# Decode attention block with MLP: V, w1 and w2 loaded through ScalarE's DMA queue, K, wq and wo through SyncE's

## The chip, the cores and the metric

The kernel runs on one core of one Trainium2 chip. The metric is the device time of one execution in microseconds. The kernel before took 678.72 us (median of 3 runs, 678.62 to 679.22). Besides these runs there is one profiled execution of 679.1 us, from which all rows below come.

## The reference

One decode step (one token for each of 4 batch entries) of a pre-layernorm transformer block: cached attention with 32 heads of 128, over 4096 cached positions, and then an MLP with mish as its activation. All inputs are bf16.

```python
# x: [4, 1, 640]; k_cache, v_cache: [4, 32, 4096, 128]; wq: [640, 4096]; wo: [4096, 640]
# w1: [640, 1728]; b1: [1728]; w2: [1728, 640]
q = layernorm(x) @ wq                              # 32 heads of 128
scores = einsum("bhqd,bhkd->bhqk", q, k_cache) * 128 ** -0.5
o = einsum("bhqk,bhkd->bhqd", softmax(scores), v_cache)
h = x + o.reshape(4, 1, 4096) @ wo
z = layernorm(h) @ w1 + b1
out = h + (z * tanh(softplus(z))) @ w2
```

The two caches are 134.2 MB each. With wq, wo, w1 and w2 the core reads 283.35 MB from HBM.

## The kernel before

The work is cut into 32 groups, numbered `g`. A group is one batch entry `b` and four heads (`g = 4 * hq + b`). Its K is one tile `kt` of 128 partitions by 32 KB, 4096 KB in all, and its V is one tile `vt` of the same size. Either pool has two buffers, so K of group g + 2 can only be loaded when K of group g has been used up, and V of group g + 1 only when V of group g - 1 has.

What happens in one group: VectorE multiplies the K tile in place with the broadcast query, in four pieces (L297, two halves of the tile called part 0 and part 1, two pieces each). TensorE sums the products over the head dimension by matmuls with the identity (L304), 8 for each piece. VectorE reduces the rest (`finish_sum`, L316). The softmax of group g - 1 lies in part 0 of group g: a maximum by VectorE (L327), a transpose by TensorE (L329), a maximum (L334), a broadcast (L342), and then on ScalarE a copy (L344) and four exponentials (L347). `pv(g - 1)`, 128 matmuls of 128x4 (L231), stands on TensorE behind part 1 of group g. So in group g the K tile of g is set free first, then the V tile of g - 1.

The order on each engine is that of the program text (a manual schedule). In the loop over the groups the loads stand in this order:

```python
        if g + 2 < NG:
            kts[g + 2] = load_k(g + 2)
        if 1 <= g < NG - 1:
            pv(g - 1)
        ...
        if g + 1 < NG:
            vts[g + 1] = load_v(g + 1)
```

All these loads are issued by SyncE, on one DMA queue, and so in this order: K of g + 2, V of g + 1, K of g + 3, and so on. The queue is called q1 in the profile. Each load waits on SyncE until its buffer is free. The K tile and the V tile of the last group (31) are loaded in two halves each. Between groups 8 and 11 the queue also takes wo in four pieces of 1280 KB (L392), in rows of 1280 bytes, and b1 (L397).

After the loop w1 and w2 are loaded (L421 to L425). They go into the K buffer that group 30 used. Then come the last softmax, `pv(30)`, `pv(31)`, the last product with wo (L278), the residual and a layernorm (L441 to L467), the product with w1 (L472, 70 matmuls, result `h1_ps`), the activation (L488 to L519), the product with w2 (L534, 70 matmuls), the transpose of the result (L549) and its store (L558).

ScalarE issues one DMA, the load of x (L101). Its other work is the copies of the query (L193, L207), the softmax and the activation.

Of the kernel before, what the change touches and what calls it, by code (L numbers as in the profile page):

```python
# [16 lines left out]
def kernel(  # L17
# [21 lines left out]
    nc = tc.nc  # L39
# [3 lines left out]
    F = B_w1.shape[1]  # L43
# [22 lines left out]
    FM = CK * CI * 128  # L66
    C2 = F // 128
# [8 lines left out]
    kpool = ctx.enter_context(tc.tile_pool(name="kpool", bufs=KBUFS))  # L76
    vpool = ctx.enter_context(tc.tile_pool(name="vpool", bufs=VBUFS))
# [2 lines left out]
    out_rows = out.rearrange("b s (c p) -> (b s c) p", p=128)  # L80


    def load_kv(pool, tag, cache, g):
        hq, b = divmod(g, N)
        t = pool.tile([128, R, Dh], BF16, tag=tag, name=f"{tag}{g}")
        view = cache[b, G * hq : G * (hq + 1)].rearrange("h (p r) d -> (h p) r d", p=PH)

        np_ = NP if g == NG - 1 else 1
        for i in range(np_):
            r0, r1 = i * R // np_, (i + 1) * R // np_  # L90
            nc.sync.dma_start(out=t[:, r0:r1, :], in_=view[:, r0:r1, :])
        return t

    def load_k(g):
        return load_kv(kpool, "kt", A_k_cache, g)

    def load_v(g):
        return load_kv(vpool, "vt", A_v_cache, g)

    x_bf = consts.tile([N, D], BF16)  # L100
    nc.scalar.dma_start(out=x_bf[:, :], in_=x_rows[:, :])  # L101
# [2 lines left out]
    nc.sync.dma_start(out=wq_sb[:, :, :], in_=A_wq.rearrange("(p c) n -> p c n", c=DC))  # L104
    kts, vts = {}, {}
    kts[0] = load_k(0)
    kts[1] = load_k(1)
    vts[0] = load_v(0)


    ident = consts.tile([128, 128], BF16)
# [22 lines left out]
    for q in range(G):  # L134
        nc.vector.tensor_copy(
            out=sel[:, :, q, q * PH : (q + 1) * PH],
            in_=ident[0:N, 0:N].unsqueeze(2).to_broadcast([N, N, PH]),
# [45 lines left out]
    def q_chunk(n):  # L183
        q_ps = ps.tile([N, QC], FP32, tag="qq")
        for c in range(DC):
            nc.tensor.matmul(  # L186
                q_ps[:, :],
                lhsT=xT[:, c, :],
                rhs=wq_sb[:, c, n * QC : (n + 1) * QC],
                start=(c == 0),  # L190
                stop=(c == DC - 1),
            )
        nc.scalar.copy(out=q_all[:, n * QC : (n + 1) * QC], in_=q_ps[:, :])  # L193

    def q_broadcast(hq):
        qb_ps = ps.tile([128, N * Dh], FP32, tag="qq")
        for b in range(N):
            for q in range(G):
                h = G * hq + q
                nc.tensor.matmul(  # L200
                    qb_ps[:, b * Dh : (b + 1) * Dh],
                    lhsT=sel[:, b, q, :],
                    rhs=q_all[:, h * Dh : (h + 1) * Dh],
                    start=(q == 0),
                    stop=(q == G - 1),
                )
        nc.scalar.copy(  # L207
            out=qbs[:, hq, :, :], in_=qb_ps[:, :].rearrange("p (b d) -> p b d", d=Dh)
        )
# [9 lines left out]
    for hq in Q_AT[-1]:  # L219
        q_chunk(hq)  # L220
        q_broadcast(hq)

    ot = {}

# [132 lines left out]
    for g in range(NG):  # L357
# [15 lines left out]
        if g + 2 < NG:  # L373
            kts[g + 2] = load_k(g + 2)
# [7 lines left out]
        if g + 1 < NG:  # L382
            vts[g + 1] = load_v(g + 1)
# [3 lines left out]
        if g in WO_AT:  # L387

            if not wo_sb:
# [3 lines left out]
                out=wo_sb[0][:, h0 : h0 + WOC, :],  # L393
                in_=A_wo.rearrange("(h p) n -> p h n", p=128)[:, h0 : h0 + WOC, :],
# [20 lines left out]
    w1_sb = w12[:, 0 : DC * F].rearrange("p (c f) -> p c f", c=DC)  # L415
    w2_sb = w12[:, DC * F :].rearrange("p (k i n) -> p k i n", k=CK, i=CI)
    w2s_sb = mlp.tile([128, D], BF16)
    w2r_sb = mlp.tile([FREM, D], BF16)

    w2_view = B_w2[0:FM, :].rearrange("(k p i) n -> p k i n", k=CK, i=CI)  # L420
    nc.sync.dma_start(out=w1_sb, in_=B_w1.rearrange("(c p) n -> p c n", p=128))  # L421
    nc.sync.dma_start(out=w2s_sb[:, :], in_=B_w2[FM : C2 * 128, :])
    nc.sync.dma_start(out=w2r_sb[:, :], in_=B_w2[C2 * 128 : F, :])
    for k in range(CK):
        nc.sync.dma_start(out=w2_sb[:, k], in_=w2_view[:, k])  # L425


    finish_sum(NG - 1, NP - 1)
# [26 lines left out]
    for dst in (h2T, hc):  # L455
        nc.vector.tensor_tensor(
            out=dst[:, :, :],
# [11 lines left out]
    for c in range(FC):  # L469
# [9 lines left out]
        if c == 4:  # L479
# [3 lines left out]
                out=std[:, :], in_=v_ps[:, :], func=ACT.Sqrt, bias=eps_t[:, :], scale=1.0  # L483
# [5 lines left out]
        out=h1n[:, :, :],  # L489
# [6 lines left out]
        out=h1s[:, :, :],  # L496
# [9 lines left out]
        out=tb[:, :, :],  # L506
# [8 lines left out]
        out=ta[:, :, :], in0=tb[:, :, :], scalar1=-0.5, scalar2=-1.0, op0=ALU.mult, op1=ALU.add  # L515
# [4 lines left out]
        out=act_t[:, :, :],  # L520
# [10 lines left out]
    for i, (w2, c) in enumerate(w2_of):  # L531
# [11 lines left out]
        out=oT[:, :, :].rearrange("p n c -> p c n"),  # L543
# [46 lines left out]
```

## Time and profile before

| | |
|---|---|
| the profiled execution | 679.1 us |
| its span, first to last instruction | 677.2 us |
| median of 3 runs | 678.72 us |
| bytes read from HBM | 283.35 MB |
| packets of q1 | 98.2% of the time of 16 DMA engines |
| TensorE matmuls | 467.1 us busy (69%) |
| VectorE | 352.9 us busy (52%) |
| ScalarE | 95.1 us busy (14%) |
| granted TensorE clock, mean | 0.769 |

Times in the traces are counted from the start of the span. "Busy" counts no DMA-issuing instructions. A DMA engine's share can come out slightly over 1.00, since the packets' times overlap a little at their ends. The 1.9 us between span and execution time lie before and after the instructions of the program.

### The profile page before, as it was taken

Reading aid. Unit: us, or ns where it says so; the run is one execution under the profiler, and the core shown is the slowest. Engines: PE = TensorE matmul, PEld = TensorE weight load, DVE = VectorE, ACT = ScalarE, POOL = GpSimd, SP = SyncE. Lnnn points to the kernel's source line nnn. Section 1 sums busy time; section 2 is a strip of 40 time slices with the busy share of each in tenths; the row PEclk is TensorE's granted clock in tenths of the full one; section 3 lists DMA queues with packets and bytes.
Section 4 is the critical chain, followed back from the end, with each engine's and each line's share of the span. In section 5 each row is a group of like instructions: output and inputs, shape, how many; then the busy total and the mean of one; then the engine's idle time right before and its main releaser. Section 6 shows DMA issues by size and latency. Waiting matters only on the chain.

```text
span 677.2 us, 12413 instructions
## 1 busy us (share of the span) xinstructions
PE 467.1 (69%) x5761; PEld 258.3 (38%) x5761; DVE 352.9 (52%) x304; ACT 95.1 (14%) x313; POOL 2.4 (0%) x13
## 2 busy tenths in 40 slices
PE   1588898787676475467677668767666776666965
PEld 0234445444333341343344434323333432333444
DVE  2476445456655356336654545665454566645722
ACT  0022112212101111011100111110011111101131
POOL 1000000000000000000000000000000000000000
PEclk9997678987667786687676788876788876767875
DMA  9999999999999999999999999999999999999993
GB/s 376 434 433 429 433 430 432 432 431 430 430 431 416 429 417 411 429 423 429 433 431 428 426 431 431 429 429 433 432 429 431 429 433 433 429 426 425 431 407 144
DMA packets 15211, 284.15 MB, mean 420 GB/s; under 512 B 1267, under 2 KB 5559, under 8 KB 6584
## 3 DMA queue, kind: packets, MB, share of 16 engines
q1 hardware_dynamic: 15152, 283.36, 98.2%
q8 instruction: 45, 0.74, 0.4%
q14 instruction: 6, 0.05, 0.0%
q10 hardware_dynamic: 8, 0.01, 0.0%
HBM read 283.35 MB, written 0.01 MB: 418 GB/s over the span
## 4 chain that ended last, share of the span: by engine, by line
DMA 66%; PE 16%; DVE 16%; issue 1%; ACT 0%; SPq 0%; DVEq 0%
DMA kt<-in_A_k_cache_dram 61%; PE s L304 14%; DVE kt L297 14%; DMA w<-in_B_w_dram 4%; DVE s_sb L316 2%; PE tr L329 1%; DVE mx L334 0%; PE h_ps L472 0%; PE y2T L534 0%; PE ot L231 0%; PE q_ps L186 0%; PE qb_ps L200 0%; ACT q_all L193 0%; DVE tb L517 0%; PE var_ps L449 0%
## 5 line engine op out<-in xcount | busy, mean ns | idle before, releaser
L304 PE MATMUL s<-kt,ident 128*128 128x512 bf16 x1024 | 299.5, 446 | 175.0 <-DVE kt L297 174.8
L297 DVE TENSOR_TENSOR kt<-kt,qbs 128x4096 bf16<-128x4096 bf16 x128 | 291.5, 2279 | 219.0 <-DMA kt<-in_A_k_cache_dram 219.0
L304 PEld LDWEIGHTS <-ident 128*128 128x128 bf16 x1024 | 107.8, 109 | 326.3 <-issue 178.4
L231 PEld LDWEIGHTS <-vt 128*128 128x128 bf16 x4096 | 109.0, 96 | 11.3 <-DMA vt<-in_A_v_cache_dram 2.2
L231 PE MATMUL ot<-e,vt 128*128 128x4 bf16 x4096 | 109.0, 165 | 4.0 <-DMA vt<-in_A_v_cache_dram 2.1
L347 ACT ACTIVATE e<-s_sb,nbs 32x128 bf16<-32x128 f32 x128 | 74.0, 578 | 2.5
L344 ACT COPY nbs<-tr 128x4 f32<-128x4 f32 x32 | 5.2, 162 | 467.3 <-PE tr L342 467.3
L316 DVE TENSOR_REDUCE s_sb<-s 128x64 f32<-128x512 f32 x64 | 43.5, 680 | 3.6 <-PE s L304 3.6
L347 ACT ACTIVATION_READ_ACCUMULATOR e<-s_sb,nbs 32x1 f32 x128 | 32.2, 252 | 0.0
L251 DVE RECIPROCAL rl<-l_ps 128x16 f32<-128x16 f32 x8 | 2.1, 257 | 45.3 <-PE l_ps L243 45.3
L334 DVE TENSOR_REDUCE mx<-tr 1x4 f32<-1x128 f32 x32 | 8.9, 279 | 30.5 <-PE tr L329 30.5
L186 PE MATMUL q_ps<-wq_sb,xT 128*4 128x512 bf16 x40 | 14.7, 517 | 9.2 <-DMA wq_sb<-in_A_wq_dram 9.2
L200 PE MATMUL qb_ps<-q_all,sel 4*128 4x128 bf16 x128 | 13.6, 286 | 5.3 <-ACT q_all L193 5.3
L329 PE MATMUL tr<-ident_f,pm 128*1 128x128 f32 x64 | 16.0, 344 | 1.2 <-DVE pm L327 1.2
L200 PEld LDWEIGHTS <-sel 4*128 4x128 bf16 x128 | 12.3, 128 | 10.7 <-issue 10.7
L193 ACT CAST q_all<-q_ps 4x512 bf16<-4x512 f32 x8 | 4.6, 574 | 74.6 <-PE q_ps L186 74.6
L342 PEld LDWEIGHTS tr<-mx,nscale 1*128 1x128 f32 x64 | 9.4, 183 | 13.8 <-issue 11.5
L329 PEld LDWEIGHTS tr<-ident_f,pm 128*1 128x1 f32 x64 | 2.8, 81 | 26.0 <-issue 26.0
L342 PE MATMUL tr<-mx,nscale 1*128 1x4 f32 x64 | 12.2, 258 | 0.4 <-DVE mx L334 0.4
L327 DVE TENSOR_REDUCE pm<-s_sb 128x1 f32<-128x128 f32 x32 | 9.2, 286 | 1.1
L186 PEld LDWEIGHTS <-xT 128*4 128x4 bf16 x40 | 3.4, 97 | 15.1 <-issue 13.5
L278 PE MATMUL yT<-otn,wo_sb 128*128 128x4 bf16 x160 | 5.5, 165 | 1.9 <-issue 1.6
(74 smaller groups left out, 51.1 us busy)
## 6 DMA issues: line engine op xcount, KB each, us to landing
kt<-in_A_k_cache_dram SPq DMA_DIRECT2D x31, 4096.0 KB, 25.7
vt<-in_A_v_cache_dram SPq DMA_DIRECT2D x31, 4096.0 KB, 32.0
wq_sb<-in_A_wq_dram SPq DMA_DIRECT2D x1, 5120.0 KB, 14.9
wo_sb<-in_A_wo_dram SPq DMA_DIRECT2D x4, 1280.0 KB, 30.7
kt<-in_A_k_cache_dram SPq DMA_DIRECT2D x2, 2048.0 KB, 23.1
vt<-in_A_v_cache_dram SPq DMA_DIRECT2D x2, 2048.0 KB
w<-in_B_w_dram SPq DMA_DIRECT2D x1, 2160.0 KB, 28.4
w<-in_B_w_dram SPq DMA_DIRECT2D x3, 640.0 KB, 19.9
```

Of the source, the lines that this page charges most:

```text
L186: nc.tensor.matmul(q_ps[:, :], lhsT=xT[:, c, :], rhs=wq_sb[:, c, n * QC : (n + 1) * QC], start=(c == 0), stop=(c == DC - 1),)
L200: nc.tensor.matmul(qb_ps[:, b * Dh : (b + 1) * Dh], lhsT=sel[:, b, q, :], rhs=q_all[:, h * Dh : (h + 1) * Dh], start=(q == 0), stop=(q == ...
L231: nc.tensor.matmul(ot[hq][:, b, :], lhsT=vt[:, r, :], rhs=e2[g % NE2][:, r, :], start=(r == 0), stop=(r == R - 1),)
L278: nc.tensor.matmul(yT[:, c, :], lhsT=wo_sb[0][:, h, c * 128 : (c + 1) * 128], rhs=otn[:, hq, :, h % G], start=(h == 0 and c == 0), stop=(h ...
L297: nc.vector.tensor_tensor(out=kt[:, :, d0 : d0 + DQ], in0=kt[:, :, d0 : d0 + DQ], in1=qbs[:, hq, b, d0 : d0 + DQ].unsqueeze(1).to_broadcas ...
L304: nc.tensor.matmul(s_ps[:, :, :], lhsT=ident[:, :], rhs=kt[:, :, d : d + W], start=(d == 0), stop=(d == Dh - W),)
L316: nc.vector.tensor_reduce(out=s_sbs[g][:, part * RP : (part + 1) * RP], in_=s_of.pop((g, part))[:, :, :], axis=AX.X, op=ALU.add,)
L327: nc.vector.tensor_reduce(out=pm[:, :], in_=s_sb[:, :], axis=AX.X, op=ALU.max)
L329: nc.tensor.matmul(tr_ps[0:1, 0:128], lhsT=pm[:, :], rhs=ident_f[:, :], start=True, stop=True)
L334: nc.vector.tensor_reduce(out=mx[:, :], in_=tr_ps[0:1, 0:128].rearrange("o (a b) -> o a b", a=G), axis=AX.X, op=ALU.max,)
L342: nc.tensor.matmul(nb_ps, lhsT=nscale[:, :], rhs=mx[:, :], start=True, stop=True)
L347: nc.scalar.activation(out=e2[g % NE2][p0:p1, :, q], in_=s_sb[p0:p1, :], func=ACT.Exp, bias=nb[p0:p1, q : q + 1], scale=SCALE, accum_out=r ...
```

## The change

`load_kv` gets the engine that issues its DMA as an argument. K stays on SyncE (`nc.sync`); V goes to ScalarE (`nc.scalar`). The loads of w1 and w2 go to ScalarE too. wq, wo, b1 and the store of the result stay on SyncE. The first V load moves in the text, from ahead of the constants to behind the first group's query (`q_chunk(0)`, `q_broadcast(0)`), so on ScalarE it stands behind the two copies of that query.

```diff
-    def load_kv(pool, tag, cache, g):
+    def load_kv(pool, tag, cache, g, dma):
...
-            nc.sync.dma_start(out=t[:, r0:r1, :], in_=view[:, r0:r1, :])
+            dma.dma_start(out=t[:, r0:r1, :], in_=view[:, r0:r1, :])
         return t
 
     def load_k(g):
-        return load_kv(kpool, "kt", A_k_cache, g)
+        return load_kv(kpool, "kt", A_k_cache, g, nc.sync)
 
     def load_v(g):
-        return load_kv(vpool, "vt", A_v_cache, g)
+        return load_kv(vpool, "vt", A_v_cache, g, nc.scalar)
...
     kts[1] = load_k(1)
-    vts[0] = load_v(0)
...
     for hq in Q_AT[-1]:
         q_chunk(hq)
         q_broadcast(hq)
+    vts[0] = load_v(0)
...
-    nc.sync.dma_start(out=w1_sb, in_=B_w1.rearrange("(c p) n -> p c n", p=128))
-    nc.sync.dma_start(out=w2s_sb[:, :], in_=B_w2[FM : C2 * 128, :])
-    nc.sync.dma_start(out=w2r_sb[:, :], in_=B_w2[C2 * 128 : F, :])
+    nc.scalar.dma_start(out=w1_sb, in_=B_w1.rearrange("(c p) n -> p c n", p=128))
+    nc.scalar.dma_start(out=w2s_sb[:, :], in_=B_w2[FM : C2 * 128, :])
+    nc.scalar.dma_start(out=w2r_sb[:, :], in_=B_w2[C2 * 128 : F, :])
     for k in range(CK):
-        nc.sync.dma_start(out=w2_sb[:, k], in_=w2_view[:, k])
+        nc.scalar.dma_start(out=w2_sb[:, k], in_=w2_view[:, k])
```

On SyncE 39 loads fall away (33 of V, 6 of w1 and w2). On ScalarE they appear in the text's order: V of g + 1 behind the four exponentials of group g - 1, and w1 and w2 between the exponentials of group 30 and those of group 31. The instructions of TensorE, VectorE and GpSimd keep their kind, number and order.

## The prediction

> **What bounds the kernel now.** I read the page's slices and queues first: are the DMA engines ever free? Columns of the queue lines: packets, MB, share of the time of 16 engines.
>
> ```profile
> DMA  9999999999999999999999999999999999999993
> q1 hardware_dynamic: 15152, 283.36, 98.2%
> q8 instruction: 45, 0.74, 0.4%
> ```
>
> They aren't. One queue, q1, keeps all 16 engines busy for 98.2% of 677.2 us. Then the table by stretch (last two columns: DMA share, GB/s), for what the engines yield:
>
> ```profile
> 40.00:180.00 140.00, 115.87 (x1294) 63.27 (x1291) 75.92 (x59) 26.20 (x77) 0.00 (x0) 0.78 1.00 431
> 200.00:300.00 100.00, 62.58 (x814) 34.70 (x813) 48.30 (x38) 12.43 (x45) 0.00 (x0) 0.76 1.01 421
> 300.00:600.00 300.00, 207.43 (x2603) 113.03 (x2602) 162.23 (x130) 37.25 (x135) 0.00 (x0) 0.76 1.00 430
> 640.00:660.00 20.00, 13.98 (x229) 8.85 (x227) 7.31 (x9) 6.46 (x20) 0.00 (x0) 0.76 0.99 409
> ```
>
> 430 GB/s where only K and V move, less where wo, w1 and w2 come in short rows. Nothing waits for SyncE's issuing as such: the loads are always ahead of the engines. So up to the last groups the time is bytes over rate, and only the order in which the last bytes arrive can add to it. That is in the chain of waits, in order of time (start, us, what):
>
> ```profile
> 614.72 20.36 DMA kt<-in_A_k_cache_dram
> 635.11 2.29 DVE kt L297
> 638.29 28.37 DMA w<-in_B_w_dram
> ...
> 671.84 2.20 PE y2T L534 x70
> ```
>
> Group 31's K is at hand at 635.1 (its first half); the chain then waits for w1, until 666.66. The compute of group 31 lies beside that wait. The timeline says how closely:
>
> ```profile
> 641.81 2.27 DVE L297 TENSOR_TENSOR kt<-kt,qbs 128x4096 bf16<-128x4096 bf16 x1
> 651.08 3.22 PE L231 MATMUL ot<-e,vt 128*128 128x4 bf16 x116
> 656.93 1.85 PE L231 MATMUL ot<-e,vt 128*128 128x4 bf16 x64
> 660.92 1.97 PE L231 MATMUL ot<-e,vt 128*128 128x4 bf16 x64 [2.15 <-DMA vt<-in_A_v_cache_dram]
> 664.95 0.17 DVE L456 TENSOR_TENSOR h2T<-hT,mean_ps 128x20 bf16<-128x20 f32 x1 [0.68 <-PE mean_ps L449]
> 666.71 0.45 PE L472 MATMUL h_ps<-h2T,w 128*128 128x4 bf16 x9 [1.79 <-DMA w<-in_B_w_dram]
> ```
>
> Part 1 of group 31 starts at 641.81; `pv(31)` waits 2.15 us for V's last half (in at 660.9); the input `h2T` of the product with w1 is ready at 665.1, and w1 comes 1.6 us later. So the compute has about 3.7 us to spare, because K of group 31 comes ahead of V of 30, V of 31, w1 and w2 in the one queue.
>
> **Part 1: 39 issues leave SyncE.** A load's issue takes 0.33 us (33 of V, 6 of weights), about 13 us. SyncE waited 382 us of its time for VectorE to free K buffers; nobody waited for it with the DMA engines empty. Worth 0. The Trainium skill ("DMA: Bandwidth & Descriptors", section "Issuing engines are not separate DMA queues") speaks against a gain: loads from several engines run on the same 16 engines and interleave, and only issue time is saved. The share of 1.00 agrees; by that rule alone the time would stay at 679.1.
>
> **Part 2: 39 issues come to ScalarE, with their waits.** V of g + 1 waits there for `pv(g - 1)`. Behind it stand the query copies of the first groups, whose matmuls stand behind the same `pv` on TensorE, and the copy L344 of the next softmax. In group 30 the exponentials end at 632.1, `pv(29)` at 637.4 and the next L344 runs at 643.74: 6 us to spare, 11 in ordinary groups. Worth 0; were the cover gone, each microsecond beyond it would delay `pv` and so the V loads, not K.
>
> **Part 3: the start.** V of 0 and 1 are issued after the second query copy, which ends at 21.1. Until then wq and half of K 0 move; K 1 is behind them. K 0, alone in at 25.4, then shares the engines and comes at about 29 to 30. The queues hold K 1, V 0 and V 1 (12.6 MB, 29 us) meanwhile and K 2 is issued 12 us after K 0 arrives, so the engines aren't empty. Worth 0, as the bytes bound.
>
> **Part 4: two queues share the engines in the groups.** Per group 8.39 MB, 19.5 us. VectorE and TensorE free a K buffer 13.7 us after they start on it (601.05 to 614.72) and the V buffer at 16.9, both under 19.5: each queue gets its next load before its present one is through. The engines stay full, and the rate is what is unknown. The nearest row is q8, instruction fetches that share an engine with q1: 0.4% of 16 x 677.2 us over 45 packets is 0.96 us for 16.4 KB, where q1's rate gives 0.62. A second queue is thus served beside the first, each slower. Bounds: all bytes at the best slice, 434 GB/s, against the mean of 426 over q1's busy 665 us would save 12 us; a loss of 1% costs 6.7. I take 0, since 430 is 1% under the best slice ever and nothing shows a loss.
>
> **Part 5: the end, where the order of arrival changes.** With one queue K 31 (4.19 MB) goes ahead of V 30. With two they go side by side, and V 30 was issued 3.2 us after K 31 (617.9 against 614.7) into a queue with no K ahead of it. At equal shares both are in when their bytes are through, which is when V 30 was in before: V 31's 4.19 MB ahead of 660.9, at about 415 GB/s (between 428 in 600:640 and 409), 10.1 us: 650.8. K's second half was in at 635.1 + 2.10 MB / 428 GB/s = 640.0. So part 1 starts at 650.8 instead of 641.81, 9.0 later. From part 1 to the w1 matmuls: 9.3 us to the end of its softmax matmul (651.08), 5.6 to the end of `pv(30)` and the row sums (656.7, with a pause of 1.9), 3.9 for `pv(31)` without its wait, 2.4 from its end (662.9) to h2T and on (665.2). Sum 21.2: the product with w1 starts at 672.0 instead of 666.7, **+5.3 us**. V 31, w1 and w2 are in by then (660.9, 666.7, and before 672.3), and the rest, 8.2 us, follows as before. Bounds: +3.4 without the pause; +7.2 if K's halves come so late that part 0 (6.7 us) holds part 1 until 652.7.
>
> **Part 6: w1 and w2 on ScalarE ahead of the last exponentials.** In SyncE's queue these six issues took from 638.29 to 653.7, with a stall of 8.96 us, behind loads ahead of them. On ScalarE w1 follows the exponentials of group 30, about 11 us after part 0 starts (644 to 646), so at 655 to 657; the exponentials of 31 are due at 650.8 + 9.4 = 660.2. The stalls had ended while V 31 still had 7 us to go; at 655 it has 6. So I expect issues of 0.4 to 0.6 us, 3 us in all, and 0 on the path. Upper bound: the whole 15.4 us again, which puts the exponentials' end at 655 + 15.4 + 2.6 = 673.0 and `pv(31)`, due at 665.7, 7.3 us later.
>
> **The sum.** 679.1 + 5.3 = 684.4 for an execution like the profiled one; that stands 0.4 over the median of 678.72, so 684.0 against the median.
>
> **The rivals.**
> - *Faster: the rate.* Two queues on each engine fill gaps between packets. For it: 421 and 409 GB/s where rows are short, 434 in the best slice. Against it: the DMA share is 1.00 now. Short rows at 430 would give 100 x 9 / 430 + 20 x 21 / 430 = 3.1 us, not enough; K and V must gain as well. It decides from a mean of 430.5 instead of 426 GB/s (7 us off 665); at 434 the time is 684.0 - 12 = 672.
> - *No change: K keeps its lead.* If the engines serve SyncE's queue first when both have work, or the change leaves the order of the last loads as it is, K 31 is in by 640 and w1 decides again: 678.7. Against it: q8's packets are served amid q1's. The Trainium skill (same page, section "Queues, rings and completion order") has the engines go round the queues, a packet from each, which speaks against a lead as well.
> - *Slower: ScalarE is held.* Part 6's upper bound: 684.0 + 7.3 = 691.3. For it: the stall of 8.96 us is there in this trace, and on ScalarE something stands behind it.
> - *Slower: V goes first.* If ScalarE's queue is preferred at the end, K's second half is in with V 31, 10.1 us later: 694. The q8 packets, with 0.96 us for 0.62, don't look preferred. A rate 1% lower gives 691 and is counted here.
>
> **How the numbers follow.** Forecast 0.55 (682 to 686 by part 5's bounds), faster rate 0.17, K's lead 0.10, ScalarE held 0.10, V first or lower rate 0.08. 0.2% (1.4 us) is about what a measurement can tell from no change. So faster 0.17, same 0.10, slower 0.73. The range takes in part of the rate rival and the held ScalarE: 676 to 692.
>
> **What would show it.** Right: two queues with some 145 and 138 MB; DMA share 1.00 and about 430 GB/s in 300:600; K 31 arriving at 648 to 652; the chain at the end running through L297, L304 and `pv(31)` instead of a wait for w1; no long idle time ahead of L347 put down to a DMA issue. Wrong: w1 again last ahead of L472; GB/s of 433 or more, or under 427, between 300 and 600; a DMA share under 0.97 there, which would mean that one queue ran dry.

## The result and the profile after

The changed kernel takes 686.66 us (median of 5 runs, 685.07 to 687.56), beside 678.79 us for the kernel before (5 runs, 678.62 to 679.22). The ratio is 1.0115, with a 95% interval of 1.010 to 1.013: slower by 7.9 us. The profiled execution is the fastest of the five, 685.07 us with a span of 683.3 us, 6.0 over the profiled execution of before.

The page's slices and queues first (queue lines: packets, MB, share of the time of 16 engines):

```profile
DMA  9999999999999999999999999999999999999992
q1 hardware_dynamic: 9088, 144.71, 50.1%
q10 hardware_dynamic: 6072, 138.65, 47.5%
```

The bytes lie on two queues now, and the engines are as full as they were: 97.6% of the time between them, of a longer span. The table by stretch (last two columns: DMA share, GB/s):

```profile
40.00:180.00 140.00, 116.73 (x1296) 63.58 (x1294) 75.12 (x58) 26.78 (x78) 0.00 (x0) 0.78 1.01 431
200.00:300.00 100.00, 53.65 (x661) 29.30 (x662) 46.47 (x40) 9.92 (x36) 0.00 (x0) 0.71 1.01 421
300.00:600.00 300.00, 211.58 (x2623) 114.67 (x2622) 167.04 (x133) 38.32 (x140) 0.00 (x0) 0.76 1.00 427
640.00:660.00 20.00, 16.08 (x197) 8.36 (x195) 13.15 (x11) 3.80 (x15) 0.00 (x0) 0.91 0.95 394
```

Up to 600 the rate hardly differs from before (430 in the third stretch there), and most of that difference is wo, whose last piece landed some 10 us later: between 300 and 340 the rate is 414 instead of 430 GB/s, from 340 to 600 it is 429 instead of 430. In that last stretch q1 had 49.8% of the engines' time and q10 49.9%. In the last row of the table VectorE is busy for 13.15 of 20 us instead of 7.31: all four pieces of group 31 fall into it, where before it held little more than the last two.

Then the timeline of the end (start, us, engine, instruction; in brackets the idle time ahead and what ended it):

```profile
629.38 2.29 DVE L297 TENSOR_TENSOR kt<-kt,qbs 128x4096 bf16<-128x4096 bf16 x1 [7.69 <-DMA kt<-in_A_k_cache_dram]
644.00 2.29 DVE L297 TENSOR_TENSOR kt<-kt,qbs 128x4096 bf16<-128x4096 bf16 x1 [2.57 <-DMA kt<-in_A_k_cache_dram]
651.42 2.29 DVE L297 TENSOR_TENSOR kt<-kt,qbs 128x4096 bf16<-128x4096 bf16 x1 [0.71 <-DMA kt<-in_A_k_cache_dram]
660.71 3.54 PE L231 MATMUL ot<-e,vt 128*128 128x4 bf16 x128
664.54 3.18 PE L231 MATMUL ot<-e,vt 128*128 128x4 bf16 x114
669.83 0.51 PE L231 MATMUL ot<-e,vt 128*128 128x4 bf16 x14 [2.11 <-issue]
672.99 0.94 PE L472 MATMUL h_ps<-h2T,w 128*128 128x4 bf16 x25 [0.63 <-DVE h_ps L467]
```

The first three rows are K of group 30, the first half of K of 31, and part 1 of group 31. Before, they started at 620.48, 635.11 and 641.81; the first of these rows was:

```profile
620.48 2.29 DVE L297 TENSOR_TENSOR kt<-kt,qbs 128x4096 bf16<-128x4096 bf16 x1 [7.73 <-DMA kt<-in_A_k_cache_dram]
```

In the changed kernel `pv(31)` no longer waits for V, and the product with w1 no longer waits for w1: it starts at 672.99 instead of 666.71, behind the compute. The chain of waits says the same (start, us, what):

```profile
624.04 27.36 DMA kt<-in_A_k_cache_dram
651.42 1.20 DVE kt L297
...
660.78 3.47 PE ot L231 x128
...
672.99 0.94 PE h_ps L472 x25
```

The wait for w1 has gone from it. From L472 on nothing has changed: 10.5 us of span remain before, 10.3 after.

### The profile page after: what moved, and what is told of

It reads as the page before. It is cut to its first block, busy times and chain, and to the rows that moved or that the text cites. A ratio compares the mean times of both kernels' runs of the same rounds, so it can differ in the third digit from the quotient of the medians.

```text
span 683.3 us, 12418 instructions
## 1 busy us (share of the span) xinstructions
PE 469.6 (69%) x5761; PEld 258.9 (38%) x5761; DVE 353.0 (52%) x304; ACT 95.0 (14%) x313; POOL 2.4 (0%) x13
## 4 chain that ended last, share of the span: by engine, by line
DMA 62%; PE 19%; DVE 16%; issue 2%; ACT 0%; SPq 0%; DVEq 0%
DMA kt<-in_A_k_cache_dram 62%; PE s L304 15%; DVE kt L297 13%; DVE s_sb L316 2%; PE ot L231 2%; PE tr L329 1%; DVE mx L334 0%; PE h_ps L472 0%; PE q_ps L185 0%; PE y2T L534 0%; PE qb_ps L199 0%; PE tr L342 0%; PE yT L278 0%; PE mean_ps L449 0%; ACT q_all L192 0%
## 5 line engine op out<-in xcount | busy, mean ns | idle before, releaser
L304 PE MATMUL s<-kt,ident 128*128 128x512 bf16 x1024 | 302.0, 448 | 181.6 <-DVE kt L297 181.3
L304 PEld LDWEIGHTS <-ident 128*128 128x128 bf16 x1024 | 108.6, 109 | 334.8 <-issue 182.2
L344 ACT COPY nbs<-tr 128x4 f32<-128x4 f32 x32 | 5.2, 162 | 475.5 <-PE tr L342 475.5
```

The lines of the kernel that those rows point to most:

```text
L304: nc.tensor.matmul(s_ps[:, :, :], lhsT=ident[:, :], rhs=kt[:, :, d : d + W], start=(d == 0), stop=(d == Dh - W),)
```

## Experiments

The theory going in was that of the prediction: the whole cost is the order in which the last loads arrive. The main rival was a cost spread over the groups, through a lower rate with two queues (427 against 430 GB/s between 300 and 600) or through ScalarE's waits. Each time below is a median, with the ratio to the kernel before and its 95% interval.

**V of 30 and 31, w1 and w2 back on SyncE** (`tail_on_sync`)

```diff
-        return load_kv(vpool, "vt", A_v_cache, g, nc.scalar)
+        return load_kv(vpool, "vt", A_v_cache, g, nc.scalar if g < NG - 2 else nc.sync)
...
-    nc.scalar.dma_start(out=w1_sb, in_=B_w1.rearrange("(c p) n -> p c n", p=128))
+    nc.sync.dma_start(out=w1_sb, in_=B_w1.rearrange("(c p) n -> p c n", p=128))
...
```

> V of groups 0 to 29 stays on ScalarE's queue; V of 30 and 31, w1 and w2 go back to SyncE's. Theory (the whole cost is the order in which the last loads arrive): K of 31 is again ahead of V of 30 in one queue, in by 642, part 1 of group 31 starts at about 643, w1 ends the chain again: 678.5 to 681 us, no more than 2 us over before. Rival (the cost is spread over the groups: a lower rate with two queues, 427 against 430 GB/s between 300 and 600, or ScalarE's waits in 30 groups): nothing comes back, 684 to 687.

Measured: 686.17 us, 1.0099 (1.0083 to 1.0115). Nothing to speak of came back. The theory failed as it stood, and the rival's number came true. The timeline of VectorE and TensorE in this run:

```profile
629.13 2.29 DVE L297 TENSOR_TENSOR kt<-kt,qbs 128x4096 bf16<-128x4096 bf16 x1 [7.69 <-DMA kt<-in_A_k_cache_dram]
638.60 4.47 DVE L297 TENSOR_TENSOR kt<-kt,qbs 128x4096 bf16<-128x4096 bf16 x2
643.91 2.28 DVE L297 TENSOR_TENSOR kt<-kt,qbs 128x4096 bf16<-128x4096 bf16 x1
650.38 2.27 DVE L297 TENSOR_TENSOR kt<-kt,qbs 128x4096 bf16<-128x4096 bf16 x1
664.63 0.46 PE L231 MATMUL ot<-e,vt 128*128 128x4 bf16 x12 [1.76 <-issue]
670.82 0.51 PE L231 MATMUL ot<-e,vt 128*128 128x4 bf16 x14 [2.27 <-issue]
```

Group 31 starts with no wait for K: the second row holds the last piece of group 30 and the first of group 31, with no idle time between them, and the two rows behind it (the second piece of part 0, the first of part 1) have no bracket either. Its K was in. But K of group 30 had come at 629.13, 8.7 us later than before. What follows waits for no load: VectorE and TensorE work through both groups, with `pv(29)` between them on TensorE, and part 1 of 31 starts 21.3 us behind the start of group 30. So the order of the last two groups was mended too late to matter.

**V of 30 issued one group later** (`late_v30`)

```diff
+        if g == NG - 2:
+            vts[g] = load_v(g)
         if 1 <= g < NG - 1:
             pv(g - 1)
...
-        if g + 1 < NG:
+        if g + 1 < NG and g != NG - 3:
             vts[g + 1] = load_v(g + 1)
```

> The changed kernel with all its loads on the same two queues; only V of group 30 is issued one group later on ScalarE, behind the exponentials of 29 and ahead of V of 31. Theory: K of 31 has the engines alone until about 642, part 1 starts near 643, and the time is 679 to 681.5 (up to 1 us of idle engines between K of 31 and V of 30). Rival (cost spread over the groups): 684 to 687. If ScalarE's w issues were what holds the end, also 684 to 687.

Measured: 686.44 us, 1.0101 (1.0084 to 1.0118). The same miss for the same reason: K of 30 at 629.67, then the compute of both groups, part 1 of 31 at 650.72 with no wait for K. The engines stood idle for longer than the 1 us expected (a share of 0.66 from 633 to 642, some 3 us), but K of 31 was in by then.

**V alone on ScalarE** (`v_only`: the change, with w1 and w2 left on SyncE)

> V on ScalarE's queue, w1 and w2 on SyncE's. Theory: K of 31 still shares the engines with V of 30 (in at about 651), and then w1 and w2 share them with V of 31, which comes at up to 670.5 instead of 661: 685 to 688.5, not better than the change. Rival that ScalarE is held by the w issues: 679 to 682, since they have left ScalarE. Rival of a cost spread over the groups: as the change, 684.5 to 687.

Measured: 686.81 us, 1.0110 (1.0096 to 1.0124). As the change itself. With no w issue left on ScalarE nothing is gained, so ScalarE isn't held by them. V of 31 sharing the engines with w1 and w2 cost nothing either: `pv(31)` waited for no load.

**w1 and w2 alone on ScalarE** (`w_only`: the kernel before, with those four lines on `nc.scalar`)

> V on SyncE's queue as before, w1 and w2 on ScalarE's behind the exponentials of group 30 (about 646). Theory: K of 31 is early as before, but w1 and w2 now share the engines with V of 30 and 31; V of 31 comes last, at 666 to 671 instead of 661, and the second half of pv(31) with it: 682 to 688. Rival of a cost spread over the groups through V: 678.5 to 680, since V is where it was.

Measured: 680.40 us, 1.0021 (1.0013 to 1.0030), 1.4 us slower. The direction is the theory's; the size is under its bounds and nearer to the rival's 678.5 to 680. TensorE's row shows the place, the second half of `pv(31)`, which waits for V 4.26 us instead of 2.15 and starts at 663.49 instead of 660.92:

```profile
663.49 1.87 PE L231 MATMUL ot<-e,vt 128*128 128x4 bf16 x64 [4.26 <-DMA vt<-in_A_v_cache_dram]
```

Sharing isn't the whole of this delay. V's last half was issued at 650.83 here, 13 us later than before (637.78): in the trace it signals its end on the semaphore of V of 30 (number 109), and SyncE waited 13.0 us for V of 30 to land.

So nearly all of the 7.9 us belongs to V. After these four runs the theory was mended: with two queues *every* K tile arrives half a group late against the bytes moved, and what counts is K of group 30, with two groups' compute behind it. The profile after has K of 28, 29 and 30 at 590.33, 609.95 and 629.38, which is 8.7, 8.9 and 8.9 us later than before, in groups of 19.4 us. The next two runs set it against the spread cost from both sides.

**One queue from V of 28 on** (`v28_on_sync`: as `tail_on_sync`, with `NG - 4` for `NG - 2`)

> As the run with V of 30 and 31 on SyncE's queue, but four groups long: V of 0 to 27 on ScalarE's queue, V of 28 to 31, w1 and w2 on SyncE's. Theory, mended: with two queues every K tile comes half a group later against the bytes moved (K of 30 at 629 to 631 instead of 620.5), and two groups' compute of 13.9 us each stands behind it; with one queue from V of 28 on, K of 29 to 31 get ahead again, K of 30 is in at about 621, part 1 of 31 starts at 642 to 643.5, and the time is 678.5 to 680.5. Rival (a cost spread over groups 0 to 27, by rate or by ScalarE's waits): 684 to 687.

Measured: 679.10 us, 1.0001 (0.9992 to 1.0009). Two groups more than in `tail_on_sync`, and the whole cost is gone. The stretch and the timeline of this run:

```profile
300.00:600.00 300.00, 210.78 (x2620) 114.40 (x2619) 165.89 (x133) 38.59 (x141) 0.00 (x0) 0.76 1.00 427
```

```profile
620.85 2.29 DVE L297 TENSOR_TENSOR kt<-kt,qbs 128x4096 bf16<-128x4096 bf16 x1 [1.89 <-DMA kt<-in_A_k_cache_dram]
641.26 2.29 DVE L297 TENSOR_TENSOR kt<-kt,qbs 128x4096 bf16<-128x4096 bf16 x1 [0.20 <-DMA kt<-in_A_k_cache_dram]
667.07 0.97 PE L472 MATMUL h_ps<-h2T,w 128*128 128x4 bf16 x25 [2.02 <-DMA w<-in_B_w_dram]
```

28 groups run here with two queues, with ScalarE's 28 issues and at the same 427 GB/s as after the change; K of 30 is in at 620.85 and w1 is the last wait again. A spread cost of more than the interval's 0.1% is refuted.

**Only the end on ScalarE** (`tail_on_scalar`: V of 30 and 31, w1 and w2 on ScalarE, V of 0 to 29 on SyncE)

> The converse: V of 0 to 29 on SyncE's queue as before, and only V of 30 and 31, w1 and w2 on ScalarE's. Theory: V of 30 jumps the queue and halves the rate of V of 29 and K of 31; K of 31 is whole at about 655, part 1 of 31 starts there, 13 us later than before, and the time is 686 to 690, more than the whole change costs. Rival of a cost spread over the groups: 678.5 to 680.5, since 30 groups are as before.

Measured: 688.84 us, 1.0145 (1.0132 to 1.0158). As the theory had it: two V loads and the weights on the other queue cost more than the whole change. Part 1 of 31 starts at 655.46, behind K:

```profile
655.46 2.29 DVE L297 TENSOR_TENSOR kt<-kt,qbs 128x4096 bf16<-128x4096 bf16 x1 [2.94 <-DMA kt<-in_A_k_cache_dram]
```

**V of 26 to 30 one group later, on two queues** (`late_v26`: as `late_v30`, for five groups)

> The changed kernel, its two queues kept for all loads; V of groups 26 to 30 is issued one group later on ScalarE (behind the exponentials of the group before it), so that K gets ahead over the last groups. Theory: K of 30 in at about 626, part 1 of 31 at 646.5 to 648 instead of 651.4, once 1 to 3 us of idle DMA engines: 680 to 683. Rival of a cost spread over the groups: 684 to 688.

Measured: 684.44 us, 1.0080 (1.0058 to 1.0101); its runs spread from 681.5 to 686.9. Over the theory's 680 to 683 and at the lower end of the rival's 684 to 688, though the rival itself is refuted by `v28_on_sync`. K of 30 and part 1 of 31 came nearly as the theory said, at 627.03 and 648.19, but from there to L472 it took 24.2 us instead of 21.6: TensorE paused twice in `pv(30)` and `pv(31)`, 2.02 and 2.54 us, where the profile after has one pause. That such pauses make up the difference in the other runs too is an inference from this one profile.

**The changed kernel again** (`after_again`)

> The changed kernel once more, for what makes its runs differ (685.1 to 687.6). Theory: the first profile shows one pause of 2.1 us of TensorE in pv(30) and pv(31), others show two; a run of 686.5 or more has two pauses of 2 us ahead of L472. Rival: part 1 of 31 starts later in such a run (652.5 or more instead of 651.4), by the rate.

Measured: 687.15 us (685.22 to 688.30), 1.0115 (1.0102 to 1.0128). The profiled execution was the one of 688.30. It has one pause (2.30 us), as has that of 685.07, so the pauses aren't what parts them. The rival's sign came, but not its reason, the rate (429 GB/s in 600:640, 426 in the first profile):

```profile
653.36 2.29 DVE L297 TENSOR_TENSOR kt<-kt,qbs 128x4096 bf16<-128x4096 bf16 x1 [4.33 <-DMA kt<-in_A_k_cache_dram]
676.23 0.94 PE L472 MATMUL h_ps<-h2T,w 128*128 128x4 bf16 x25 [0.63 <-DVE h_ps L467]
```

Part 1 of 31 waits 4.33 us for the second half of K and starts 1.9 us later than in the other profile. Behind it another 1.3 us are lost: the last 16 matmuls of L304 take 5.7 us from first to last instead of 4.7, at a granted clock of 0.74 instead of 0.89 (651 to 664). So L472 starts 3.2 us later, which is the difference in time. V of 31 was issued at 644.09 instead of 646.61, in both profiles as `pv(29)` ended, and `pv(29)` came earlier because K of 30 did (627.69 instead of 629.38). An earlier K of 30 thus brings V of 31 onto the engines earlier, beside K's last half. That this is what delayed K's last half fits the times, but no run tests it alone.

**Queues exchanged** (`mirror`: K, w1 and w2 on ScalarE, V, wq and wo on SyncE)

> The changed kernel with the queues exchanged: K, w1 and w2 on ScalarE's, V, wq and wo on SyncE's. Theory (the engines serve both queues alike): K of 30 at 627.5 to 631, part 1 of 31 at 650.5 to 653.5, 684 to 688.5. Rival (SyncE's or ScalarE's queue is preferred): K of 30 earlier than 626 or later than 634 and a time under 682 or over 691.

Measured: 687.63 us, 1.0131 (1.0114 to 1.0147). The time and part 1 of 31 (652.73) are as the theory said. K of 30 isn't: it came at 623.95, ahead of the theory's 627.5 and earlier than the 626 that was the first half of the rival's sign. The other half, a time under 682 or over 691, didn't come: V of 31 was issued at 640.87, and the wait for K of 31 took the lead back (6.84 us ahead of part 1). From 340 to 600 the queues had 49.5% (K) and 50.3% (V) of the engines' time. There is no sign that one queue is worth more than the other; why K of 30 came earlier stays open.

**One queue, K behind V** (`k_behind_v`: the kernel before, `load_k(g + 2)` moved behind `load_v(g + 1)`; `last_k_behind_v`: the same for groups 27 to 29 alone)

```diff
-        if g + 2 < NG:
-            kts[g + 2] = load_k(g + 2)
         if 1 <= g < NG - 1:
             pv(g - 1)
...
             vts[g + 1] = load_v(g + 1)
+        if g + 2 < NG:
+            kts[g + 2] = load_k(g + 2)
```

> The kernel before, one queue on SyncE for everything; only the order of the two loads in the loop is exchanged: V of g + 1 first, then K of g + 2. Theory (order of arrival alone, no second queue and no issue on ScalarE needed): K of 30 comes behind V of 29, at 629 to 631.5 instead of 620.5, the last two groups' compute follows late, and the time is 684 to 688. Rival (two queues on the engines, or loads on ScalarE, cost something themselves): 678.5 to 680.5, as neither is there.

Measured: 707.75 us, 1.0423 (1.0403 to 1.0443), far over the expectation. This run can't tell order from supply: K is now issued behind `pv`, 3.6 us later, and the engines weren't always full (a share of 0.98, and 409 instead of 430 GB/s between 300 and 600):

```profile
300.00:600.00 300.00, 201.55 (x2464) 108.03 (x2464) 159.69 (x128) 37.00 (x135) 0.00 (x0) 0.75 0.98 409
```

> The kernel before, one queue on SyncE for everything; the two loads of the loop are exchanged for groups 27 to 29 alone, so that K of 29, 30 and 31 come behind V of 28, 29 and 30, and the queue can run short three times at most (about 1 us each, by the run with the exchange in all groups). Theory (order of arrival alone): K of 30 at 629 to 633, part 1 of 31 at 652 to 655, 684.5 to 690. Rival (a second queue or loads on ScalarE are needed for the loss): 678.5 to 681.5.

Measured: 688.10 us, 1.0134 (1.0117 to 1.0151). K of 30 at 630.12 and part 1 of 31 at 652.53, with everything on one queue and ScalarE out of it. The queue runs short here too: from 621 to 630 the share is 0.64, which is some 3 us of idle engines ahead of K of 30 and so about a third of its delay of 9.6 us. Up to 600 the rows are those of before. The loss needs neither a second queue nor loads on ScalarE; K behind V in the last groups is enough. That a smaller delay costs too is shown by `late_v26`, which lost 5.4 us with K of 30 at 627.03.

## Why the prediction was right, and where its step fell short

The forecast of 684.0 us, slower with a chance of 0.73, missed the median by 2.7 us and lies inside the stated 676 to 692. Against the profiled execution it was 684.4 for 685.07.

- *Parts 1 to 3 (issues off SyncE, issues on ScalarE, the start): worth 0.* Right: `v28_on_sync` has nearly all of these changes and takes the time of before. K of group 0 came sooner than due, at 26.74 instead of 29 to 30.
- *Part 4 (the rate): worth 0.* Right. The trace shows 427 instead of 430 GB/s between 300 and 600, just at the mark under which the step would have been wrong, but most of that is wo's later landing (429 instead of 430 from 340 on), and `v28_on_sync` takes the time of before with the same 427.
- *Part 5 (the end).* Numbers right, reason incomplete. Part 1 of 31 was due at 650.8 and started at 651.42; from there to L472 21.2 us were due and 21.6 took place; together 6.3 instead of 5.3. But the step put the delay down to K of 31 sharing the engines with V of 30 alone. `tail_on_sync` and `late_v30` gave K of 31 its lead back and gained nothing. K of 30 was late as well, by 8.9 us (629.38 against 620.48), for the same sharing one group earlier, and the compute of groups 30 and 31 behind it (21.25 us in `tail_on_sync`) reaches part 1 of 31 at 650.6 on its own. In this execution two limits nearly coincide, 650.6 and 651.42, and the step named only the second; that the number came out although one of two limits was missing is luck. Its bound of +7.2, drawn from part 0, would have been the place to look at group 30. The equal shares didn't hold at this place either. The queue lines of the profile after for 633 to 645:

```profile
q10 hardware_dynamic: 111, 3.44, 66.5%
q1 hardware_dynamic: 118, 1.67, 32.7%
```

  V of 30, in rows of 32 KB, had two thirds of the engines' time, and K of 31, loaded in halves and so in rows of 16 KB, one third. In `mirror`, with the queues exchanged, it was 61.5% for V and 33.6% for K, so this went with the tiles and not with the queues. V of 30 was through at 645.4 instead of together with K at 650.8, and K's last half then shared the engines with V of 31.
- *Part 6 (ScalarE held): worth 0.* Right. The six issues ran from 653.79 to 658.92, and the next copy L344 at 660.82 waited for TensorE. `v_only`, without them, is no faster.
- *The rest of the median's difference*, 1.6 us over the profiled execution, is the spread of the changed kernel's runs. Of the two profiles of it, the slower has K's last half 1.9 us later and 1.3 us more behind it. What moves K of 30, and with it the issue of V of 31, from run to run stays open.
- *The rivals.* A higher rate didn't come. K kept no lead: the engines served both queues, 49.8 and 49.9% of their time from 340 to 600, which fits the late K of 30. The Trainium skill's rule ("DMA: Bandwidth & Descriptors", section "Queues, rings and completion order") of going round the queues fits it too. The Trainium skill's rule that several issuing engines only save issue time ("DMA: Bandwidth & Descriptors", section "Issuing engines are not separate DMA queues") holds for the bytes: the last row of w1 was in at 666.6, against 666.2 before. By itself it would have given 679.1, and the measured 685.07 shows what it leaves out, the order in which tiles are complete.

## What to carry to other kernels

With the DMA engines full, the second queue brought no bytes sooner here; it changed which tile was complete first. A single queue that loads the tile with the long compute behind it ahead of the one that is needed later is a schedule. Split over two queues, the tiles shared the engines and every K came later; the loop had room for that, and the end, with the compute of two groups behind the last whole K, had none. To test whether two queues cost anything in the loop itself, join them again some groups before the end, far enough for the order to recover: two groups were too few here, four gave everything back.

## What the runs showed of the hardware beyond what was expected

- Two queues with rows of 32 KB shared the engines evenly: 49.8 and 49.9% of their time from 340 to 600, at 429 GB/s together. Rows of 16 KB beside rows of 32 KB got 32.7% against 66.5%, as one row from each queue in turn would give.
- That doesn't hold for w1 and w2: in `w_only` their rows of 1280 to 5120 bytes had 60.1% of the engines' time beside V's 36.2% from 648 to 654, and 24.6% beside 75.6% from 654 to 660. What sets these shares was not tested.
- A load can be held by the landing of another that signals on the same semaphore: 13.0 us for V's last half in `w_only`. Which loads share one differed from run to run of this series, without being part of any edit.
- On one queue, V and K issued together at 605.71 and 606.13, while the K ahead of them had still some 4 us to go (in at 609.70), already yielded 5% less (409 against 430 GB/s). By the share of 0.98 the engines were idle for 2% of the time; the rest is a lower rate while busy. Why wasn't tested.
- TensorE pauses of 0.9 to 2.8 us inside `pv(30)` or `pv(31)`, which the profile puts to "issue", come once or twice at the end, and count only where the compute is the last wait. The 13 profiles have 18 of them, and each ends 1.3 to 1.5 us behind the end of a fetch of 16 KB of instructions (queue q8); in the profile after the fetch ends at 668.4 and the pause at 669.83. No run tests whether the fetch is the cause.
